# A DeltaNet layer and an MLP on one core: masked copies on half the columns, W1 in narrower pieces, masks in wide operations, and a new order

## The chip, the cores and the metric

The kernel runs on one core of a Trainium2 chip. The core has five engines that run side by side, each through its own list of instructions in order: PE (TensorE, matrix products), DVE (VectorE), ACT (ScalarE), POOL (GpSimd) and SP, which here only issues DMAs. ACT and POOL issue DMAs too. An engine that waits for a semaphore holds up everything behind it in its own list. The metric is the device time of one execution in microseconds; lower is better. Before the change the median of three runs is 508.97 us (507.42 to 509.17).

## The reference, cut to what matters

```python
def _attn_ref(q, k, v, beta):            # B, H, S, D = 4, 8, 768, 48
    k_n = k / (np.linalg.norm(k, axis=-1, keepdims=True) + 1e-06)
    state = np.zeros((B, H, D, D))
    for t in range(S):
        kt, vt, bt = k_n[:, :, t], v[:, :, t], beta[:, :, t, None]
        y[:, :, t] = np.einsum('bhd,bhde->bhe', q[:, :, t], state)
        v_old = np.einsum('bhde,bhd->bhe', state, kt)
        state = state + bt[..., None] * np.einsum('bhd,bhe->bhde', kt, vt - v_old)
    return y

def _moe_ref(x, g_ln, w_ch1, w_ch2):     # x: (4, 768, 384)
    mu, var = mean and variance of x over the last axis
    xn = (x - mu) / np.sqrt(var + 1e-06) * g_ln
    return x + np.maximum(xn @ w_ch1, 0.0) @ w_ch2
```

The 32 heads' outputs of the first part, side by side, are the rows of 384 that the second part takes. `w_ch1` (384 x 1536) and `w_ch2` (1536 x 384) come as 64-bit floats, all else as 32-bit floats.

## The kernel before, in words

The 768 steps of the recurrence are cut into 12 chunks of 64 (C). Within a chunk the recurrence becomes matrix work: with G, the products of the chunk's keys among themselves (`gram`), scaled by beta and the norms, the chunk needs the inverse of a triangular 64x64 matrix for each of the 32 heads (xt). Then `recur` computes the chunk's updates u, its outputs y and the new state, normalises the rows of y (`ln_act`) and transposes them (xnt). `mlp` multiplies by W1, applies the maximum with zero and multiplies by W2; from chunk 1 on the second product, and from chunk 4 on the first too, use schemes with fewer products and more sums (`seven`, `fifteen`).

The inverses are made in two ways. For chunk 0 `first_inverse` does it in six levels of doubling. Heads are taken in two groups g. Level 0 scales G by the factors ndb (L693) and puts its masked elements into a matrix that starts as a copy of the unit matrix (L702, `copy_predicated`), which is transposed on DVE (L708) and copied by ACT (`back`, L679). Each further level n has a product E (L720, 32 products of 64x64), a masked copy of E out of PSUM into another such matrix (L727, mask n), a product Z (L737), transposes of Z (`nat`, L685) and copies of its changed columns (`back`). In level 5 alone E, Z and the masked copy work on half of the columns. For later chunks `rows_inverse` does it by a loop of 31 steps on DVE, each a product and a difference (L856, L863), after its G has gone to DRAM (gd) and come back regrouped (gb), followed by a store (xd), loads of the blocks (xt) and `join`. Chunk 1 has its own loop; from then on two chunks share one.

The masks of the six levels are made in the first microseconds from two iotas, on 64-wide tiles: four operations for xor, eye and rows, and for each level two on the bits (L395, L402) and one that joins them (L408). `first_norms` makes ndb from the squares of k: a sum (L595), a square root (L596), +1e-6 (L597), a product (L598), a reciprocal (L599) and a scaling (L602).

W1 and W2 are loaded as pairs of 32-bit words in 12 pieces of 768 KB on ACT's queue (`fetch`) and turned into 32-bit floats by `convert`: two operations on ACT (L524, L532), a shift on DVE (L529) and a sum on POOL (L542). A piece of W1 is 128 rows by 768 columns, so that a tile of 128 columns of W1 needs three pieces. The first three pieces are converted in halves.

The order of all work is written out: `Line.add` numbers each step, the string ORDER lists the numbers, and each engine's list and each DMA queue follow it. What an engine does next is never decided on the chip.

## Time and profile before

| what | value |
|---|---|
| median of three runs | 508.97 us |
| the profiled execution's own time | 506.83 us |
| its span, first to last instruction | 505.1 us |
| PE busy | 485.9 us (96%) |
| DVE, POOL, ACT busy | 355.2, 275.7, 249.0 us |
| chain that ended last | PE 78%, DVE 13%, SP's queue 3% |
| first L1322 (first product of MLP 0) | 53.1 us |
| rows loop of chunk 1 on DVE | 39.98 to 72.2 us |

Busy times overlap between engines. The clock in the profile is the share of full speed that PE was granted; a group of 32 products of 64x64 takes 0.69 us at full clock and about 1.1 at half. "L693" is a line of the kernel before; durations of single instructions come from the timeline of the one profiled execution.

### The profile page before, as it was taken

The page shows a single profiled execution, that of the slowest core. Times are in us where ns is not written, and L with a number is a line of the kernel's source. Part 1 is how long each engine was busy: PE and PEld are TensorE (multiplying, and loading weights), DVE is VectorE, ACT ScalarE, POOL GpSimd, SP SyncE. Part 2 cuts the span into 40 slices and gives each one's busy share as a digit, 9 for nine tenths or more (in the row PEclk, how much of TensorE's full clock was granted, in tenths as well). Part 3 has the DMA queues.
Part 4 walks back from the last instruction along what each step waited for, and adds up shares of the span by engine and source line. Part 5 has one row for each costly group of instructions (what it writes and reads, how often), then busy time and mean ns, then how long its engine had stood idle before and what let it go on. Part 6 is the DMA issues. An engine that isn't in the chain of part 4 may idle for free.

```text
span 505.1 us, 22184 instructions
## 1 busy us (share of the span) xinstructions
PE 485.9 (96%) x9606; PEld 445.7 (88%) x9606; DVE 355.2 (70%) x774; ACT 249.0 (49%) x620; POOL 275.7 (55%) x430
## 2 busy tenths in 40 slices
PE   6777999999999999999999999999999999999996
PEld 3666988688988898899999999999999999999996
DVE  9689987997699458886559898478899238143251
ACT  5777772633645434636444544436563347363230
POOL 5464527255754595629893462591642851645643
PEclk9776799999999999999999999999999999999999
DMA  8979896756646676448734434765245412111101
GB/s 173 308 153 187 270 189 79 107 138 133 90 87 106 192 127 114 46 100 205 155 41 64 102 55 153 150 91 87 57 85 136 82 23 58 43 50 46 31 12 31
DMA packets 196097, 54.99 MB, mean 109 GB/s; under 512 B 186076, under 2 KB 189404, under 8 KB 196000
## 3 DMA queue, kind: packets, MB, share of 16 engines
q1 hardware_dynamic: 189920, 40.58, 42.1%
q10 hardware_dynamic: 3872, 9.83, 6.1%
q0 software_dynamic: 2208, 3.17, 3.7%
q8 instruction: 75, 1.23, 1.0%
q14 instruction: 22, 0.18, 0.1%
HBM read 36.64 MB, written 16.91 MB: 106 GB/s over the span
## 4 chain that ended last, share of the span: by engine, by line
PE 78%; DVE 13%; SPq 3%; issue 2%; POOL 1%; DMA 1%; ACT 1%; ACTq 0%; DVEq 0%; POOLq 0%
PE f L1419 31%; PE f L1217 22%; PE f L1296 6%; DVE xb L863 4%; DVE tmp L856 4%; SPq L349 3%; PE by L1020 2%; PE two L1013 2%; PE by L979 2%; PE by L771 2%; PE two L979 2%; PE two L1030 1%; PE two L771 1%; PE by L894 1%; PE by L900 1%
## 5 line engine op out<-in xcount | busy, mean ns | idle before, releaser
L1406 POOL TENSOR_TENSOR h_all<-h_all 128x256 f32<-128x256 f32 x123 | 90.2, 746 | 133.3 <-PE f L1419 103.7
L1419 PE MATMUL f<-w_sb,h_all 128*128 128x192 f32 x492 | 109.5, 332 | 0.0
L1419 PE MATMUL f<-words,h_all 128*128 128x192 f32 x396 | 84.5, 330 | 0.3 <-POOL h_all L1406 0.3
L1419 PEld LDWEIGHTS f<-w_sb,h_all 128*128 128x128 f32 x492 | 81.8, 190 | 1.8 <-DVE o L1437 0.2
L863 DVE TENSOR_TENSOR xb<-xb,tmp 128x87 f32<-128x87 f32 (+21 forms) x186 | 73.7, 396 | 4.8
L856 DVE TENSOR_TENSOR tmp<-xb,gb 128x87 f32<-128x87 f32 (+21 forms) x186 | 73.1, 393 | 4.9
L1237 DVE TENSOR_TENSOR h_all<-h_all,f 128x512 f32<-128x512 f32 x96 | 63.6, 682 | 14.2 <-PE f L1217 13.1
L1419 PEld LDWEIGHTS f<-words,h_all 128*128 128x128 f32 x396 | 66.6, 190 | 1.7 <-POOL h_all L1406 1.0
L1296 PE MATMUL f<-xnt,w_sb 128*128 128x256 f32 x216 | 50.2, 382 | 0.0
L349 POOL DMA_DIRECT2D tb<-in_k_dram x64 | 41.9, 660 | 10.3 <-DVE kt L751 9.4
L1239 ACT ACTIVATE h_all<-h_all 128x512 f32<-128x512 f32 x48 | 28.5, 624 | 34.4 <-DVE h_all L1237 34.0
L1296 PEld LDWEIGHTS f<-xnt,w_sb 128*128 128x128 f32 x216 | 40.2, 190 | 5.2
L1233 ACT COPY h_all<-f 128x512 f32<-128x512 f32 x48 | 26.3, 590 | 33.9 <-PE f L1217 17.1
L1437 DVE TENSOR_TENSOR o<-f,x 128x192 f32<-128x192 f32 x33 | 11.6, 352 | 41.8 <-PE f L1419 25.9
L1217 PE MATMUL f<-words,w_sb 128*128 128x128 f32 x256 | 31.7, 276 | 0.0
L1305 ACT ACTIVATE h_all<-f 128x256 f32<-128x256 f32 x36 | 13.4, 383 | 34.8 <-PE f L1296 34.8
L1217 PEld LDWEIGHTS f<-words,w_sb 128*128 128x128 f32 x256 | 30.0, 192 | 0.2
L1217 PE MATMUL f<-xnt,w_sb 128*128 128x128 f32 x192 | 25.4, 276 | 0.0
L542 POOL TENSOR_TENSOR w_sb<-words 128x768 uint32<-128x768 uint32 (+1 forms) x11 | 15.0, 1364 | 17.7 <-DVE words L529 16.7
L1217 PEld LDWEIGHTS f<-xnt,w_sb 128*128 128x128 f32 x192 | 23.7, 192 | 0.1
L1322 PEld LDWEIGHTS f<-xnt,w_sb 128*128 128x128 f32 x144 | 19.5, 203 | 3.4 <-ACT h_all L1330 0.2
L1084 ACT ACTIVATE xnt<-xnt,g_sb 128x256 f32<-128x256 f32 x27 | 12.5, 499 | 19.2 <-DMA xnt<-xld 19.1
(246 smaller groups left out, 955.0 us busy)
## 6 DMA issues: line engine op xcount, KB each, us to landing
words<-in_moe_w_ch_dram ACTq DMA_DIRECT2D x10, 768.0 KB, 7.8
gd<-gsb SPq DMA_DIRECT2D x11, 512.0 KB, 3.9
v<-in_v_dram SPq DMA_DIRECT2D x24, 192.0 KB, 4.2
kr<-in_k_dram SPq DMA_DIRECT2D x46, 96.0 KB, 3.9
out_dram<-o SPq DMA_DIRECT2D x44, 96.0 KB, 2.4
xld<-xlt SPq DMA_DIRECT2D x9, 384.0 KB, 3.0
xnt<-xld SPq DMA_DIRECT2D x36, 96.0 KB, 3.3
gb<-gd SPq DMA_DIRECT2D x44, 64.0 KB, 3.0
```

Source lines behind the costliest of these rows:

```text
L349: add(eng, cost, lambda: QUEUE[eng].dma_start(out=out_, in_=in_), r, w, bulk=n * ns / 16e3, **kw)
L856: lambda j=j, n=n, w=w, t=t: nc.vector.tensor_tensor(out=t, in0=xv[:, 0:n, j : j + 1].to_broadcast([np_, n, w]), in1=gv[:, j : j + 1, j + ...
L863: "DVE", dve(n * w), lambda t=t, rest=rest: nc.vector.tensor_tensor(out=rest, in0=rest, in1=t, op=ALU.subtract),
L979: nc.tensor.matmul(dst[half(e), hp, j], src[drows(hp), (e if n else key_half(c, hp, e)) * GP + j], s_all[drows(hp), e, j], start=(n == 0 o ...
L1217: nc.tensor.matmul(wide(p[:, 128 * n : 128 * n + 128]), w[n // 2][:, n % 2 * 128 : n % 2 * 128 + 128], r, start=start and n == 0, stop=Tru ...
L1233: add("ACT", act(512), lambda: nc.scalar.copy(o, p), pk, ok)
L1237: add("DVE", dve(512), lambda: nc.vector.tensor_tensor(out=o, in0=o, in1=p, op=op), pk, ok)
L1239: add("ACT", act(512), lambda: nc.scalar.activation(o, o, ACTF.Relu), [], ok)
L1296: nc.tensor.matmul(p[:, 0:TOK], w1_sb[:, t, f * 128 : (f + 1) * 128], xnt[:, t], start=(t == 0), stop=(t == KC - 1))
L1322: nc.tensor.matmul(p[:, 0:128], w1_sb[:, t, f * 128 : (f + 1) * 128], xnt[:, t, cols], start=(t == 0), stop=(t == KC - 1))
L1406: add(eng, cost, lambda: e.tensor_tensor(out=out_, in0=x, in1=y, op=op), r, w, port=2 if eng == "Pool" else 1, pr=-2)
L1419: lambda f=f, t=start and f == 0: nc.tensor.matmul(p[:, 0:D2], lhs(f), rhs[:, f], start=t, stop=(f == F2 - 1), skip_group_check=True),
```

## The change

Five things. (1) The masks: the bits of xor and of the row or column number are packed into one word (`both`), shifted by all levels' amounts at once, masked and compared. Mask 0 and masks 1 to 5 are each made in three operations, the packing takes two: 8 where there were 18, and one of the four before them goes, against a small iota on POOL. (2) In levels 2 to 4 E is computed, and the masked copy made, only on the half of the columns that the level changes; the copy is then two instructions, one for each PSUM bank. Z stays whole. (3) A piece of W1 is all 384 rows by 256 columns, so that one piece holds all of two tiles of 128 columns; its rows in DRAM are 2 KB long. (4) In `first_norms` the squared norm is made by ACT (Square with bias 1e-6), beside DVE's +1e-6. (5) ORDER is new from the first step to the last.

```diff
+    c_pool(lambda: nc.gpsimd.iota(steps, pattern=[[1, 6]], base=0, channel_multiplier=0), 0.15, ["steps"])
...
-    for n in MASKED:
-        k_, m, w = n, masks[n], C
-        t1, t2 = (flat[:, C * i : C * i + w] for i in (2 * n, 2 * n + 1))
+    for n, (own, key) in enumerate(((bits, "bits"), (rows_, "rows"))):
         c_dve(
-            lambda t1=t1, k_=k_, w=w: nc.vector.tensor_scalar(
-                out=t1, in0=xor[:, 0:w], scalar1=w - 1, scalar2=k_, op0=ALU.bitwise_and, op1=ALU.logical_shift_right
+            lambda n=n, own=own: nc.vector.scalar_tensor_tensor(
+                out=both[:, n], in0=own, scalar=16, in1=xor, op0=ALU.logical_shift_left, op1=ALU.bitwise_or
             ),
...
+    for n in range(2):
+        ns_ = slice(0, 1) if n == 0 else slice(1, 6)
+        m_ = ns_.stop - ns_.start
         c_dve(
...
+            lambda n=n, ns_=ns_, m_=m_: nc.vector.tensor_tensor(
+                out=wide[:, ns_], in0=both[:, n : n + 1].to_broadcast([128, m_, C]),
+                in1=steps[:, ns_, None].to_broadcast([128, m_, C]), op=ALU.logical_shift_right,
             ),
...
+                out=wide[:, ns_], in0=wide[:, ns_], scalar1=65536 + C - 1, scalar2=None, op0=ALU.bitwise_and
...
+                out=small[:, ns_].bitcast(I32), in0=wide[:, ns_], scalar1=65537, scalar2=None, op0=ALU.is_equal
...
+    WC = WN // KC
     pieces = [
-        (w1_sb[:, t, f : f + WN], w_ch1.bitcast(U32)[t * 128 : (t + 1) * 128, 2 * f : 2 * (f + WN)], ("w1", t, f // WN))
-        for f in range(0, DFF, WN)
-        for t in range(KC)
+        (
+            w1_sb[:, :, f : f + WC],
+            w_ch1.bitcast(U32)[:, 2 * f : 2 * (f + WC)].rearrange("(t p) n -> p t n", p=128),
+            ("w1",),
+        )
+        for f in range(0, DFF, WC)
...
+            add("ACT", 0.21, lambda nr=nr, nd=nd: nc.scalar.activation(nd, nr, ACTF.Square, bias=eps), kn_ + ["eps"], kd, **kw)
             add("DVE", 0.17, lambda nr=nr: nc.vector.tensor_scalar_add(nr, nr, 1e-6), [], kn_, port=2, **kw)
-            add("DVE", 0.17, lambda nr=nr, nd=nd: nc.vector.tensor_tensor(out=nd, in0=nr, in1=nr, op=ALU.mult), kn_, kd, port=1, **kw)
...
         def cols(ap, n, x):
-            return ap.rearrange("p a i (b x l) -> p a i b x l", x=2, l=1 << n)[:, :, :, :, x] if n == 5 else ap
+            if n == 5:
+                return ap.rearrange("p a i (x l) -> p a i x l", x=2)[:, :, :, x]
+            return ap[:, 0].rearrange("p i (b x l) -> p i b x l", x=2, l=1 << n)[:, :, :, x] if n >= LEAST else ap
...
         def col2(ap, n, x):
-            return ap.rearrange("p (b x l) -> p b x l", x=2, l=1 << n)[:, :, x] if n == 5 else ap
+            return ap.rearrange("p (b x l) -> p b x l", x=2, l=1 << n)[:, :, x] if n >= LEAST else ap
...
-                for nr, v, pk in E[4]:
+                for nr, v, pk in E[4] if n < LEAST or n == 5 else [
+                    (slice(a, a + 1), v[:, a - nr.start : a - nr.start + 1], E[2 + a]) for nr, v, _ in E[4] for a in range(nr.start, nr.stop)
+                ]:
```

The numbers in ORDER are step numbers, which the new steps shift, so its lines can't be compared as they stand. Matched by what the steps are, these are the moves that the prediction speaks of:

- ACT: the first fetch of W1 stands right after the two k loads (before: after three copies and two squares), and the first conversion of that piece (L524) right after the squares of k, ahead of the square root, of both copies of kt (L573) and of all else. The fetches of the second and third piece stand after those copies.
- DVE: the pads and masks come first, with the wide shift just before the first sum of squares (L595); both groups of level 0 are scaled, copied and transposed before masks 1 to 5 are compared, and then both level-1 copies follow each other. The shift of W2's first piece (L529) stands ahead of the level-5 copy of group 1 (before: behind u's scaling).
- PE: both G products, then G of chunk 1, then E of level 1 for both groups and Z for both; both E and both Z of level 2 and E of level 3 stand ahead of the first queries product (L771). The second y product and two transposes of chunk 3's keys stand ahead of the first product of MLP 0.
- POOL: W2's first piece is summed ahead of the second half of W1's second piece.
- SP: six loads of q for chunk 2 stand behind the store of xd and the loads of gb (before: ahead of them). The xd store keeps its place between gb loads.
- From chunk 2 on every engine's list has swaps of neighbouring steps; the steps are the same.

74 lines of the change are left out of this document (37 added, 37 removed), and 184 rows, old and new, of the table ORDER.

## The prediction

> **What bounds the kernel now.** I read the page's slices first, then the windows of 10 us, then the chain and the timeline of the opening.
>
> ```profile
> PE   6777999999999999999999999999999999999996
> DVE  9689987997699458886559898478899238143251
> PEclk9776799999999999999999999999999999999999
> ```
>
> PE is full from the fifth slice (50 us) on and has holes before it; its clock is below full only there. The windows give the size:
>
> ```profile
> 0.00:10.00 10.00, 6.95 (x58) 3.47 (x58) 8.98 (x31) 4.18 (x10) 6.60 (x17) 1.00 0.84 137
> 10.00:20.00 10.00, 7.66 (x207) 6.32 (x207) 7.36 (x20) 8.36 (x21) 1.71 (x3) 0.74 1.12 305
> ...
> 40.00:50.00 10.00, 7.69 (x224) 6.87 (x228) 8.76 (x30) 7.85 (x20) 5.13 (x6) 0.60 0.93 166
> 50.00:60.00 10.00, 9.97 (x211) 8.99 (x204) 9.69 (x19) 8.02 (x19) 4.79 (x4) 0.72 0.88 294
> ...
> 150.00:200.00 50.00, 50.00 (x1140) 44.61 (x1133) 34.54 (x82) 20.62 (x54) 33.68 (x54) 1.00 0.66 132
> ```
>
> Of PE's 19.2 us idle (505.1 - 485.9), 14 us lie before 50 us; later there are 0.4 us at 123 us, about 0.3 until 150, and 4.4 after 400, nearly all of it the last sums and stores. So the end moves by as much as the opening does, if PE is then still fed. It is fed through DVE: the chain runs over DVE's rows loop (L856, L863) from 53 to 114 us, then SP's eight DMAs and `xnj` at 123.03, for which PE waits only 0.4 us. A lead must therefore exist on both: PE's opening work, and the point where the rows loop of chunk 1 stands.
>
> Inside the opening, the chain and the timeline:
>
> ```profile
> 3.88 3.28 DVE xb L402 x2
> ```
> ```profile
> 5.93 0.52 ACT L594 ACTIVATE xln<-kr 128x384 f32<-128x384 f32 x1 [2.18 <-DMA kr<-in_k_dram]
> 7.04 0.37 ACTq L349 DMA_DIRECT2D words<-in_moe_w_ch_dram  x1
> 8.10 0.54 DVE L595 TENSOR_REDUCE ksum<-xln 128x8 f32<-128x384 f32 x1
> 11.15 0.68 DVE L693 TENSOR_TENSOR gsb<-two,ndb 128x512 f32<-128x512 f32 x1
> 15.16 0.55 ACT L524 ACTIVATE words<-words 128x384 f32<-128x384 f32 x1
> 18.23 0.76 DVE L727 COPY_PREDICATED gsb<-u,by 128x512 f32<-128x512 int32 x1
> 42.10 0.43 DVE L727 COPY_PREDICATED pt<-u,two 128x256 f32<-128x256 int32 x1
> ```
>
> The squares of k end at 6.45, yet DVE reduces them at 8.10, behind mask work: 1.65 us late. The first scaling of G (L693) comes at 11.15; the second level-1 copy (L727, group 1) ends at 18.99. The last level, already on half the columns, takes 0.43 instead of 0.73.
>
> **The change part by part.** *Masks.* Twenty-two DVE instructions become eleven, and POOL gets one more iota (0.17, L375; its order now has it ahead of the beta DMAs, hidden in the first 2 us). A 64-wide operation has 0.20; the 320-wide ones lie between 64 and larger rows: shift 0.47 (0.21 at 64, 1.24 at 1024), and and compare 0.30 each (0.20 at 64, 0.32 at 384). Together some 2.9 us, against some 7.8 us of busy DVE now, since several were stretched (L402 2.38, L395 1.47). On the path: up to -1.65 for the reduce. At worst nothing, where another wait takes its place.
>
> *Predicated copies, levels 2 to 4.* Six of 0.73 (512 elements) become twelve of 128. The line through 0.73 at 512 and 0.43 at 256 gives 0.28 at 128, so 0.56 a pair: -0.17 each, -0.5 on the chain of one group. Bounds: if short runs of 4 to 16 columns cost what 256 do (0.43), +0.13 each, +0.8 over six; at 0.16, the small operation's row, -0.4 each. I take -0.5, since level 5's row is the same operation.
>
> *E on half the columns.* Nothing: level 5's 32 products of 64x32 took 1.09 and 1.08, the 64x64 ones at the same half clock 1.08. At full clock the 64x64 group takes 0.69 and its weight loads 0.56, so at best -0.13 each.
>
> *Norms.* The multiply (0.16) leaves DVE, a Square (0.2 to 0.3, as L596) joins ACT; the +1e-6 (0.17) leaves the path. Zero, within 0.2.
>
> *W1 in pieces.* Same bytes, same count of fetches and conversions, rows of 2 KB instead of 6. The first fetch moves from 7.04 to ACT's place right after the k loads (about 2.2), and its first conversion (L524) moves ahead of the square root and the two kt copies on ACT. ACT waits there until the whole piece has landed, and behind it wait the norms, PE's first Gram products and so L693. Landing now takes 6.5 to 9.2 us (the `words` rows), so 8.7 to 11.4; then L524 0.55, sqrt 0.3, two kt copies 0.56 with small steps between: PE's Gram product at 10.9 to 13.6, done 0.69 later, and L693 at 11.6 to 14.3 instead of 11.15. The eight k loads and two q loads share the DMA engines with it, already at 1.1 in 4 to 7 us. MLP's own need of W1 starts at 53 us: hidden, with 10 us to spare for pieces 0 and 2; piece 1's second half now follows a W2 piece (1.49) on POOL, near 50, so with 2 us of cover.
>
> *Reordering, level 0 and 1.* Both groups are scaled, copied and transposed before E: 0.68+0.75+0.65+0.73+0.70+0.70 = 4.2 us, then the mask compare 0.3, then both level-1 copies 1.5 with no PE work between. From L693: 6.0 us. Before it was 7.8 (11.15 to 18.99), because Z1, slow at half clock, and G of chunk 1 stood between the E products. So the second copy ends at 17.6 to 20.3, against 18.99: -1.4 to +1.3.
>
> *Reordering, levels 2 to 5.* Z2 of both groups and E3 now stand ahead of the queries product, which held PE for 2.4 us ("issue", 22.17 to 24.58). I follow ACT, which carries the back copies and the W1 conversions: from words0's landing (fetch now at about 13, so 19.7 to 22.3) six back copies, two q copies and a conversion put Z2 at about 24 (24.8 now). Z2 1.1, two transposes 0.8, E3 1.1, then on DVE copy 0.28, W1 shifts 0.33 and 0.55, copy 0.28: Z3 at 28.7 (32.1 now). Z3 1.1 and transposes 0.8; on DVE two scalings of P 1.34, two copies 0.56, a shift 0.55, a copy 0.28, the norms 0.9, a copy 0.28: Z4 at 34.5 (37.1 now). Then the gb scaling and four transposes, 3.1: the loop's first step at 37.6 (39.98 now). But DVE then has a W2 shift (L529, 0.55) ahead of the last level's second copy, and that shift waits for ACT's Prelu, which stands behind the back copies of Z4 and Z5: about 44.1. Behind the shift are the copy, Z5 of group 1 and u. So u's scaling ends near 46.2 (47.5), y0 begins at 46.2 (47.56), and the loop's step of 192 elements is at 46.9 (47.42). What is lost there was won before.
>
> *After the opening.* DVE's rows loop keeps its count; one W2 shift (0.55) now lies before this point rather than after it, another moves behind the loop, and an xnt scaling (0.54) moves into it: net -0.4, so the loop ends 0.9 early. After it, SP's store and seven gb loads (72.2 to 76.9) still end the wait, with the q loads now behind them: 0. PE meanwhile has done the second y0 and two transposes (0.68 and 1.04, 1.7 us of work) before MLP rather than after. From 125 us on the order is new as well; that can hardly win where idle is near zero, and costs 0 to 1.5 (three waits like the 0.58 at 492).
>
> **Sum:** the loop's lead of 0.9 and the 1.4 of y0 pull at the same PE; between them, since some PE work now lies ahead of the loop's results, I take the mean, and the later order at zero: **-1.2 us**. The profiled execution then is 505.6 (now 506.83 = span 505.1 + 1.73); the median stands 2.14 above it, so **507.8 us** against 508.97. The half-percent bound, about what a measurement of this kernel can tell from no change, is 2.5 us.
>
> **The two behaviours behind the spread.** Stretched L402 (2.38, others 0.13 to 0.20) overlaps three POOL copies of 0.62 (L421). The new wide shift stands just ahead of the reduce, with three such copies queued on POOL: if it is stretched like that, 1.9 us, the reduce is no earlier than now. That costs the forecast nothing, as ACT is held to 8.7 anyway, but takes 1.65 from case (a) below. The Trainium skill, "SBUF — State Buffer", Who interferes with whom, says that a VectorE operation with two SBUF inputs and a GpSimd one that reads SBUF exclude each other for a whole instruction; by that rule the stretch would come.
>
> The granted clock is 0.5 at 15 to 21.5, 25 to 31.5 and 42.5 to 55.6 us, in the last spell with PE busy in every microsecond from 48: 7.6 us of dense work before full clock. The Trainium skill, "TensorE: Matmul & The Clock Gate", The HAM clock gate, says that about 3.4 us of sustained work bring it back; by that rule the new kernel's spell would end some 4 us after its dense work begins, and the time would be that of case (c), early; the trace shows it slower.
>
> **The rivals.**
> (a) *The opening gains in full.* The W2 shift isn't late (Prelu ready by 42), so the 2.4 us at the loop's first step survive, with the 0.55 of that shift, done early; if the piece lands early too, the reduce's 1.65 comes on top: -3 to -4.6, 504.4 to 506. For it: the lead at Z3 of 3.4 us; against: ACT is full from 24 to 38 by the sum of its rows.
> (b) *ACT held by the first W1 piece.* Slower than before: the piece contends with the small k and q packets; landing at 11.4 or later gives +1.3 at level 1, delays words0 and everything behind ACT by as much again: +2.6, and +4 with the 1.5 of the later order: 511.6 to 513. It decides from a landing at 10.1 us, 7.9 after issue; the median of the rows is 7.8. Against: landings that long had two other pieces beside them.
> (c) *Clock.* The last half-clock spell ends sooner or later than the opening's lead would have it. For it: the spells before lasted 6.5, so they vary from 6.5 to 13; against: the same operations, in groups of the same size. Half of that difference either way, 3.3 us at half speed, is 1.7 us of PE work: 506.1 (early) or 509.5 (late).
> (d) *Nothing arrives.* The loop, not PE, sets the end, and its lead is lost to stretched steps (L863 1.57, L856 1.55 now): 509.
>
> **How the numbers follow.** Forecast with (d), whose time is inside its range: 0.42. (a) 0.29. (b), with losses in the new later order: 0.20. (c) early 0.05, late 0.04. Of the forecast, 0.02 lies more than 2.5 us slower, by waits after 125. So faster 0.29 + 0.05 = 0.34, same 0.40 + 0.04 = 0.44, slower 0.22. The likeliest case alone: 506.5 to 509.5. The range of 8 in 10 leaves out the best of (a) and the worst of (b), a tenth each: 504.6 to 511.9.
>
> **What would show it.** Right: the reduce at 6.5 to 7; L693 at 11.6 to 12.5; second level-1 copies ending at 17 to 18.5; 128x128 predicated copies at 0.25 to 0.30; E of 64x32 no shorter than weight loads; PE idle before 50 us near 13 us. Wrong: ACT idle over 3 us before its first L524; the wide shift over 1 us; PE idle in 100 to 130 us; a half-clock spell past 57 us; waits of over 1 us between 130 and 490.

## The result, and the profile after

The changed kernel takes **512.39 us** (median of 20 runs, 509.37 to 516.31) against 508.99 us (20 runs, 505.85 to 510.75): a ratio of 1.0075, 95% interval 1.0058 to 1.0092. It is slower by 3.4 us. The forecast was 507.8, its range ended at 511.9; the time that came is that of rival (b), 511.6 to 513. The profiled execution took 511.42 us, 1 us under its median, with a span of 509.6 us, 4.5 more than before's 505.1.

The page's slices (40 equal parts of the span, tenths busy; the last row is the granted clock):

```profile
PE   5758899998999999999999999999999999999996
DVE  3787896997789539987749898559989336244251
PEclk9985999999899999999999999999999999999999
```

The first slice shows a late start: DVE at 3 where it had 9, PE at 5 where it had 6. The windows of the profile after (busy us of PE, weight loads, DVE, ACT and POOL with counts in brackets, then clock, DMA share, GB/s):

```profile
0.00:10.00 10.00, 4.43 (x13) 1.78 (x13) 2.33 (x13) 4.52 (x7) 6.48 (x19) 1.00 0.84 163
40.00:50.00 10.00, 8.23 (x194) 7.07 (x190) 7.02 (x22) 6.12 (x15) 4.49 (x5) 0.55 1.01 210
50.00:60.00 10.00, 8.03 (x330) 7.13 (x324) 9.66 (x23) 8.54 (x23) 5.67 (x8) 1.00 0.78 218
125.00:150.00 25.00, 22.89 (x654) 21.02 (x655) 18.40 (x44) 12.97 (x38) 9.90 (x16) 0.93 0.56 78
```

In the first 10 us DVE works 2.33 us (8.98 before) and PE runs 13 products (58 before). PE is idle for 25.6 us in all, 19.2 before; 1.97 of it now lie in 50 to 60 us and 2.11 in 125 to 150, where there were 0.03 and 0.27. PE's busy time is 1.9 us less: the opening's last half-clock spell ends near 49 us rather than at 55.7, mean clock 0.983 against 0.973. So rival (c)'s early clock came in this execution, and bought nothing: PE waited instead. It was this execution's luck: over all 20 executions the mean clock has a median of 0.976 (0.961 to 0.986), and over 31 of the kernel before, run beside the first experiments, 0.975 (0.964 to 0.978). A new half-clock spell of 3.4 us lies at 127.6 to 131.0 (the 0.93 in the last window, 1.00 before).

The loss starts in the opening. Its timeline (start, duration, engine, line, operation, count; in brackets the idle time before it and what ended it; ACTq and SPq are DMA issues):

```profile
0.80 7.83 SPq L349 DMA_DIRECT2D kr<-in_k_dram  x7
2.25 0.64 ACTq L349 DMA_DIRECT2D h_all<-in_moe_w_ch_dram  x1
9.38 0.94 ACT L605 ACTIVATE xln<-kr 128x384 f32<-128x384 f32 x2 [2.53 <-DMA kr<-in_k_dram]
9.66 0.39 PE L590 MATMUL f<-ident,u 16*64 16x8 f32 x6 [2.85 <-DMA u<-in_beta_dram]
9.93 0.55 DVE L606 TENSOR_REDUCE ksum<-xln 128x8 f32<-128x384 f32 x1 [6.59 <-ACT xln L605]
10.22 0.54 ACT L542 ACTIVATE h_all<-h_all 128x384 f32<-128x384 f32 x1
15.41 0.69 DVE L706 TENSOR_TENSOR gsb<-by,ndb 128x512 f32<-128x512 f32 x1 [1.43 <-PE by L646]
21.17 0.74 DVE L742 COPY_PREDICATED gsb<-u,two 128x512 f32<-128x512 int32 x1 [0.63 <-PE two L733]
```

The first piece of W1 is issued at 2.25. SP's seven k loads take 7.83 us to issue (5.10 for the same seven in the run late_fetch below, which has that fetch later), the squares of k begin at 9.38 instead of 5.93, and the transposes of k on PE stand behind the beta products, which wait for beta until 9.66. The conversion of the piece (L542, at 10.22) shows no wait of its own: by then the piece had landed. What came late was k and beta.

"Step 192" below is the loop's step of 192 elements on DVE; `xnj` is the second transpose of that name, that of chunk 2's inverse (the first, chunk 1's, is at 83.78 before and 85.83 after). Both are starts.

| stage (us) | forecast | before | after |
|---|---|---|---|
| reduce of the squares of k | 6.5 to 7 | 8.10 | 9.93 |
| first scaling of G (L693, now L706) | 11.6 to 14.3 | 11.15 | 15.41 |
| second level-1 copy ends | 17.6 to 20.3 | 18.99 | 21.91 |
| Z2 | 24 | 24.8 | 26.24 |
| Z3 | 28.7 | 32.1 | 30.81 |
| Z4 | 34.5 | 37.1 | 37.20 |
| first step of chunk 1's loop | 37.6 | 39.98 | 39.38 |
| level-5 copy, group 0 | | 42.10 | 42.06 |
| W2 shift (L529, now L547) | 44.1 | | 47.89 |
| u's scaling begins | | 46.94 | 49.19 |
| y0 (L1020, now L1035) | 46.2 | 47.56 | 50.17 |
| step 192 | 46.9 | 47.42 | 50.60 |
| chunk 1's loop ends | | 72.16 | 73.96 |
| `xnj` | | 123.03 | 126.28 |
| span less `xnj` | | 382.1 | 383.3 |

Against the forecast the chain is 1.8 to 2.7 us late from Z2 to the loop's first step and 3.7 late at step 192. Against the kernel before it has made up the late start by Z3, and the loop's first step and the level-5 copy of group 0 are as early as before. The 3.2 us at step 192 arise between 42 and 50.6 us. Four lines show where, three of the kernel after and, last, the back copies of late_fetch:

```profile
42.06 0.44 DVE L742 COPY_PREDICATED pt<-u,two 128x256 f32<-128x256 int32 x1 [0.34 <-PE two L733]
43.28 0.83 ACT L692 COPY xt<-f 64x128 f32<-64x128 f32 x3 [2.73 <-POOL w_sb L553]
47.89 0.56 DVE L547 TENSOR_SCALAR words<-words 128x768 uint32<-128x768 uint32 x1 [1.94 <-ACT words L542]
```

```profile
41.02 0.83 ACT L692 COPY xt<-f 64x128 f32<-64x128 f32 x3
```

ACT stands 2.73 us in front of a W2 fetch, with back copies of the inverse behind it. The list names POOL's sum, but in the trace's records the fetch counts on the same semaphore (number 107) as a k load that SP issued at 34.44; that load lands at 42.71, and ACT's wait for the semaphore ends at 42.73. Behind the back copies stands ACT's Prelu, for which DVE's W2 shift waits 1.94 us; behind the shift are the level-5 copy of group 1, u, and the loop's steps. In late_fetch SP issued that load at 32.06, and ACT issued the fetch at 39.72 without a wait.

After step 192 the difference falls to 1.8 us at the end of chunk 1's loop, is 3.25 at `xnj`, and 1.2 more come behind it. Differences of this size in single traces must be read with care: new_to_130 below has the changed kernel's order up to 125 us and an `xnj` at 125.34, 0.9 us earlier; old_to_130 and old_order, with one order up to there, are 1.5 apart (123.00 and 124.48). At step 192 these pairs agree within 0.3 us.

### The profile page after: what moved, and what is told of

It is laid out like the page before. It is cut to its first block, busy times and chain, and to the rows that moved or that the text cites. A ratio compares the mean times of both kernels' runs of the same rounds, so it can differ in the third digit from the quotient of the medians.

```text
span 509.6 us, 22168 instructions
## 1 busy us (share of the span) xinstructions
PE 484.0 (95%) x9606; PEld 443.4 (87%) x9606; DVE 352.5 (69%) x767; ACT 250.2 (49%) x623; POOL 278.7 (55%) x431
## 4 chain that ended last, share of the span: by engine, by line
PE 82%; DVE 5%; DMA 4%; ACT 3%; POOL 3%; issue 2%; SPq 1%; ACTq 0%; POOLq 0%; DVEq 0%
PE f L1434 30%; PE f L1232 22%; PE f L1311 6%; PE f L1337 3%; PE by L1035 2%; PE two L994 2%; PE two L1028 2%; PE by L786 2%; DVE tmp L871 2%; PE by L994 2%; PE f L1352 2%; PE two L1045 2%; PE two L786 1%; DVE xb L878 1%; SPq L349 1%
## 5 line engine op out<-in xcount | busy, mean ns | idle before, releaser
L1434 PE MATMUL f<-words,h_all 128*128 128x192 f32 x396 | 87.4, 333 | 0.3 <-POOL h_all L1421 0.3
L871 DVE TENSOR_TENSOR tmp<-xb,gb 128x87 f32<-128x87 f32 (+21 forms) x186 | 76.2, 410 | 4.6
L878 DVE TENSOR_TENSOR xb<-xb,tmp 128x87 f32<-128x87 f32 (+21 forms) x186 | 75.1, 404 | 4.5
L1311 PEld LDWEIGHTS f<-xnt,w_sb 128*128 128x128 f32 x216 | 40.1, 190 | 5.4 <-ACT xnt L1122 0.4
L1232 PE MATMUL f<-words,w_sb 128*128 128x128 f32 x256 | 32.4, 277 | 0.0
L1232 PEld LDWEIGHTS f<-words,w_sb 128*128 128x128 f32 x256 | 30.2, 192 | 0.3
L1232 PE MATMUL f<-xnt,w_sb 128*128 128x128 f32 x192 | 25.1, 275 | 0.0
L1232 PEld LDWEIGHTS f<-xnt,w_sb 128*128 128x128 f32 x192 | 23.5, 192 | 0.1
L1208 POOL TENSOR_TENSOR words<-xnt 128x128 f32<-128x128 f32 x32 | 15.3, 486 | 13.8 <-ACT xnt L1099 13.7
```

Source lines behind the costliest of these rows:

```text
L871: lambda j=j, n=n, w=w, t=t: nc.vector.tensor_tensor(out=t, in0=xv[:, 0:n, j : j + 1].to_broadcast([np_, n, w]), in1=gv[:, j : j + 1, j + ...
L878: "DVE", dve(n * w), lambda t=t, rest=rest: nc.vector.tensor_tensor(out=rest, in0=rest, in1=t, op=ALU.subtract),
L1208: "Pool", 0.47, lambda: nc.gpsimd.tensor_tensor(out=o, in0=x, in1=y, op=op), xk + yk, ok,
L1232: nc.tensor.matmul(wide(p[:, 128 * n : 128 * n + 128]), w[n // 2][:, n % 2 * 128 : n % 2 * 128 + 128], r, start=start and n == 0, stop=Tru ...
L1311: nc.tensor.matmul(p[:, 0:TOK], w1_sb[:, t, f * 128 : (f + 1) * 128], xnt[:, t], start=(t == 0), stop=(t == KC - 1))
L1434: lambda f=f, t=start and f == 0: nc.tensor.matmul(p[:, 0:D2], lhs(f), rhs[:, f], start=t, stop=(f == F2 - 1), skip_group_check=True),
```

## The experiments

The runs are read by step 192, `xnj`, and span less `xnj`. The medians are over all executions of a run; "before" is the kernel before on the same chip in the same batch.

### The place of the first fetch, from both sides: early_fetch and late_fetch

early_fetch is the kernel before with its own first W1 fetch (6 KB rows) moved right behind ACT's k loads, and nothing else:

```diff
 L349 DMACopy kr_89<-in_k_dram 64x8x48 x2
+L349 DMACopy words_66<-in_moe_w_ch_dram 128x1536
 ...
 L573 TensorCopy kt_72<-by 128x4x2x64
-L349 DMACopy words_66<-in_moe_w_ch_dram 128x1536
```

> The kernel before with one thing moved: its own first W1 fetch, 768 KB in rows of 6 KB, stands right behind the two k loads of ACT (about 2.2 us) instead of at 7.04. Theory A (the place of the fetch, not the form of the piece): the squares of k start at 8 to 9.5 us instead of 5.93, L693 at 13 to 14.5 instead of 11.15, and the time rises by 1.5 to 3.5 us, to 510.5 to 512.5. Rival D (the pieces of 256 columns do it, three times as many rows of 2 KB): the squares stay at 6 to 6.8, the time within 0.7 of 509.0. Rival B (a lag in the opening is caught up with): squares late, time within 0.7 of 509.0.

late_fetch is the changed kernel with that fetch moved back behind the first copy of kt, and the piece's three conversions moved back too, behind back copies of level 0:

```diff
 L349 DMACopy kr_89<-in_k_dram 64x8x48 x2
-L349 DMACopy h_all<-in_moe_w_ch_dram 128x3x512
 ...
 L605 Activation xln<-kr_89 128x384 x2
-L542 Activation h_all<-h_all 128x3x128
 L607 Activation knrm_121<-ksum_119 128x8
 L584 TensorCopy kt_72<-by 128x4x2x64
+L349 DMACopy h_all<-in_moe_w_ch_dram 128x3x512
```

> The changed kernel with one thing moved: the first W1 fetch stands behind the first kt copy on ACT instead of right behind the k loads, and the three conversions of that piece (two Prelu, one multiply) stand behind the back copies of level 0. Theory A (the early fetch holds up the k and beta loads on the DMA engines, and the opening's lag comes from there): the squares of k start at 5.9 to 6.5 us instead of 9.38, the first scaling of G (L706) at 11 to 12.5 instead of 15.41, the second level-1 copy ends at 17.5 to 19 instead of 21.91; the time falls to 508 to 510.5, as far as a later hold at 40 to 48 us lets the lead through. Rival B (the opening's lag is caught up with anyway and the loss of 3.4 us arises after 40 us): L706 comes as early, but u and y0 (49.19 and 50.17 us) move by under 0.7 us and the time stays at 511.5 to 512.5. Rival C (it is the conversion on ACT ahead of the norms, not the loads): the squares stay at 9.4.

early_fetch: 510.40 us against 509.06 (ratio 1.0052, 1.0015 to 1.0089), span 507.3. late_fetch: 510.76 against 509.06 (1.0027, 0.9998 to 1.0055), span 507.8. The squares of k in the timeline, of early_fetch first and then of late_fetch:

```profile
9.08 0.53 ACT L594 ACTIVATE xln<-kr 128x384 f32<-128x384 f32 x1 [4.64 <-DMA kr<-in_k_dram]
```

```profile
6.37 0.94 ACT L605 ACTIVATE xln<-kr 128x384 f32<-128x384 f32 x2 [0.19 <-DMA kr<-in_k_dram]
```

One moved DMA instruction delays the squares from 5.93 to 9.08 in the old kernel, and moving it back, with the conversions, brings them from 9.38 to 6.37 in the new one. The DMA views of the first 10 us of the kernel after and of late_fetch (count, size, median us from issue to landing) say the same of k:

```profile
kr<-in_k_dram SPq DMA_DIRECT2D x7, 96.0 KB, 6.8
```

```profile
kr<-in_k_dram SPq DMA_DIRECT2D x7, 96.0 KB, 4.0
```

PE's wait for beta ends at 7.19 in late_fetch and at 9.66 in the changed kernel.

What this costs is known less well than that it happens. In ratios the early place costs the old kernel 0.52%, 2.6 us (0.8 to 4.5 by the interval), and the late one gives the new kernel 1.0075 - 1.0027 back, 2.4 us of the 3.8 that the ratio makes. By medians it is 1.3 and 1.7: three of early_fetch's ten executions took 513.8 to 515.7 us, the others 509.0 to 511.1. early_fetch has W1 in the old pieces, so it isn't their form.

Nor does the delay go through whole. In early_fetch 3.15 us at the squares are 1.75 at the loop's first step (41.73) and 1.5 at step 192 (48.95). In late_fetch the lead over the changed kernel is 3.05 us at the first scaling (12.36) and 1.6 at the end of level 1 (20.28), after a pause of PE of 2.06; at Z2 (26.24), Z3 (31.02), Z4 (37.75) and the loop's first step (39.93) there is none. At u (47.80) and step 192 (49.24) it is 1.4 again, since ACT's wait before the W2 fetch has gone.

The Trainium skill, "DMA: Bandwidth & Descriptors", Queues, rings and completion order, says that each DMA engine takes its queues in turn, a packet of some 9 to 17 descriptors from one before it goes to the next; with 768 KB in large rows in one queue and k in rows of 192 bytes in another, that goes with what is seen here (k lands 6.8 us after issue beside it, 4.0 without). How the engines share their time within a load isn't in these traces.

### The rest of the opening: late_beta, hold_fix, repaired

late_beta is late_fetch with the transposes of k ahead of the beta products on PE:

```diff
 L568 Matmult f_132<-u 128x512 x2
+L579 Matmult by<-ident,kr_89 128x128 x8
 L590 Matmult f_129<-ident,u 64x8
 ...
-L579 Matmult by<-ident,kr_89 128x128 x8
```

> As the run late_fetch, and besides PE's eight small products of beta stand behind the eight k transposes of chunk 0 instead of ahead of them. Theory M (in the changed kernel PE waited at 9.66 for beta, which comes over POOL's queue, before it took k, so that the place of these products is a second reason for the late start): the k transposes start at 6.0 to 6.8 instead of 7.51 in late_fetch, the first scaling of G (L706) at 10.8 to 11.8 instead of 12.36, the time falls by 0.4 to 1.2 us against late_fetch, to 509.6 to 510.4. Rival N (the start is then set by the kt copies on ACT or by the norms on DVE): L706 at 12 to 12.6, the time within 0.4 of late_fetch's 510.76.

510.77 us against 508.56 (1.0041, 1.0020 to 1.0063), span 509.4: nothing won, although the opening did what was hoped. The transposes of k came at 6.30 (7.51 in late_fetch), the first scaling at 10.21, and the second level-1 copy ended at 18.25, 0.74 ahead of the kernel before. The loop's first step was still 1.7 ahead (38.28). ACT stood twice:

```profile
19.22 0.57 ACT L542 ACTIVATE words<-words 128x384 f32<-128x384 f32 x1 [2.81 <-DMA words<-in_moe_w_ch_dram]
41.60 0.83 ACT L692 COPY xt<-f 64x128 f32<-64x128 f32 x3 [2.24 <-DMA tb<-in_k_dram]
```

At 16 us it stands in front of a conversion whose piece hasn't landed; that was made up. At 39 us it stands in front of the W2 fetch that waits for SP's k load (landed 41.03, wait ended 41.05, semaphore 107 again), with back copies (L692) behind, and u came at 47.51, 0.6 later than before, step 192 at 48.92, 1.5 later. PE was idle 5.4 us less than in the changed kernel but busy 5.1 us more, with the clock at half from 24.3 to 55.0.

hold_fix takes the changed kernel as it is and mends only 40 to 50 us:

```diff
 ACT
-L349 DMACopy words_68<-in_moe_w_ch_dram 128x2x768
 ...
 L692 TensorCopy xt_84<-by 128x4x2x16
+L349 DMACopy words_68<-in_moe_w_ch_dram 128x2x768
 DVE
+L742 CopyPredicated pt_79<-u,by 128x2x4x32
 ...
+L1016 TensorTensor u<-two,bnat 128x2x4x48
 L547 TensorScalarPtr words_67<-words_67 128x768
 ...
-L742 CopyPredicated pt_79<-u,by 128x2x4x32
-L1016 TensorTensor u<-two,bnat 128x2x4x48
```

E of level 5 for group 1 also goes ahead of a group of key transposes on PE.

> The changed kernel, its first fetch left early; reordered only between 40 and 50 us: on ACT the back copies of level 4 of both groups go ahead of a W2 fetch; on PE E5 of group 1 goes ahead of the kt transposes of chunk 2; on DVE the last level's second copy and u's scaling go ahead of the W2 shift, and POOL's addition follows that shift. Theory A2 (this stretch adds a hold of its own to the opening's lag): ACT's idle 2.7 us at 40.5 goes, Z5 of group 0 starts at 42 to 43 instead of 43.93, u's scaling at 46.3 to 47.6 instead of 49.19, and the time falls by 1 to 2.2 us, to 510.2 to 511.4. Rival E (what was put back makes the W2 additions and the later fetches late, or DVE's rows loop sets the end whatever u does): u is early, but the time stays within 0.6 of 512.4.

513.20 us against 509.06 (1.0068, 1.0037 to 1.0099), span 511.6: no gain. k was late again (squares at 8.47). The hold itself went: from Z4 to u it took 10.2 us instead of 12.0. But Z4 came 2.0 later (39.22), so that u was at 49.37, and the moved W2 shift now stood between u and the loop's next steps: from u to step 192 it took 3.04 us, 1.41 in the changed kernel. Why Z4 came later isn't settled.

repaired puts together late_beta, the W1 conversions behind Z1's back copies, the W2 fetch behind Z4's, E of level 5 earlier, and the W2 shift behind step 192.

> The run late_beta with two more edits to its order. First, the four W1 conversions that stand on ACT between level 0 and level 1 go behind Z1's back copies and the q copies, and their two shifts on DVE behind the level-2 copies; in late_beta ACT stood 2.8 us at 19.2 for a piece to land. Second, Z4's back copies of both groups go ahead of the W2 fetch (ACT stood 2.24 us at 41.6 behind that fetch, which itself waited for a k load to land), E5 of group 1 goes ahead of the kt transposes, and the W2 shift goes behind the loop's step of 192. Theory S (these two holds on ACT are what eats the lead that late_beta had at 18 us, 0.74 us ahead of the kernel before): E2 at 20.5 to 21.5 instead of 22.95, u's scaling at 44.5 to 46.5 instead of 47.51, the step of 192 at 45.5 to 47.5 instead of 48.92, the time 507 to 509.2. Rival T (the work put back comes due at once on another engine, or PE's issue stalls and half clock take the lead): u after 46.8 or the step of 192 after 48, the time over 509.8.

510.74 us against 509.55 (1.0031, 1.0012 to 1.0050), span 507.5. u came at 46.80, as early as before (46.94), step 192 at 48.00, the best of the new order but 0.6 us behind the kernel before, and `xnj` at 124.50. Before 30 us PE stood 2.49, 1.50 and 0.91 us with no releaser but "issue".

Z4 to u is the stretch that holds the wait for the W2 fetch. It took 12.0 us in the changed kernel, 12.1 in new_to_130 and 11.4 in late_beta, which have that wait; 10.1 in late_fetch, 10.2 in hold_fix and 10.7 in repaired, which don't; 9.8 in the kernel before.

### The parts by themselves: masks_halves, masks_halves_late, halves_only, pieces_only

masks_halves is the kernel before, in its own order and with its own W1 pieces, with the wide masks and the half-column E and copies.

> The kernel before, with the wide bit masks (in its own order, each wide step where the first of the old ones stood) and with E and the predicated copies of levels 2 to 4 on half of the columns, each copy as two of 128 elements in one place; W1 pieces, fetches, norms and all the rest of the order as before. Theory F (these two parts are good for what the forecast gave them, and the loss comes from the W1 fetch and the order): the reduce of ksum at 6.5 to 7.2 instead of 8.10, L691's first scaling of G 0.5 to 1.5 us earlier than 11.15, copies of 0.27 to 0.30; the time 506.8 to 508.6. Rival G (the parts gain nothing, since other waits take their place: the kt copies on ACT, the queries product's stall): 508.6 to 509.5. Rival H (they cost, by broadcast reads that stretch beside POOL or by the second copy's own overhead): over 509.8.

510.52 us against 509.06 (1.0023, 0.9993 to 1.0053), span 509.2. The reduce came at 6.74, as the prediction wanted for the masks, and yet the first scaling of G fell from 11.15 to 13.67. The timeline of masks_halves:

```profile
9.89 3.04 DVE L604 TENSOR_SCALAR knrm<-knrm 128x8 f32<-128x8 f32 x1
9.95 0.94 POOL L838 MEMSET xb<- 64x1024 f32 x1 [2.32 <-DVE u L415]
10.00 2.92 DVE L606 RECIPROCAL ndb<-ndb 128x8 f32<-128x8 f32 x1
10.85 1.16 POOL L428 COPY xt<-u 128x512 f32<-128x512 f32 x2
11.95 0.94 POOL L1547 MEMSET tb<- 128x1024 f32 x1
```

POOL waits for the last mask, since the masks' scratch tile is the one that it clears for the rows loop. With the masks done early it clears at 9.95 rather than at 18.29, and an addition on 8 elements a row takes 3.04 us instead of 0.16: it ends, with the reciprocal, when POOL's four instructions in a row are done. masks_halves_late tests this by one move on DVE:

```diff
 L604 TensorScalarPtr knrm_121<-knrm_121 128x8
-L415 TensorScalarPtr u<-xb 128x320
 L605 TensorTensor ndb<-knrm_121 128x8
 ...
 L711 CopyPredicated kt_74<-u,gsb_80 128x2x256
+L415 TensorScalarPtr u<-xb 128x320
 L738 CopyPredicated gsb_82<-u,two 128x2x256
```

> The kernel before with the wide masks and the half-column copies and E, as in the run masks_halves, but with one step moved: the compare that finishes masks 1 to 5 stands just ahead of the first level-1 copy instead of between the small steps of the norms. POOL's clearing of xb waits for that compare, and behind it stand two copies and another clearing. Theory I (in masks_halves POOL's 3 us of work, set free at 9.9 us, stood beside the norms' small DVE steps and stretched an addition and a reciprocal to 3 us): these steps take 0.2 us each, the first scaling of G (L702) starts at 9.8 to 11 us instead of 13.67, the time falls to 507 to 508.8. Rival J (the stretch has another cause, or the order of the rows loop takes the gain back): L702 stays over 12.5, or the time stays at 509.5 to 510.5.

508.04 us against 508.56 (0.9990, 0.9963 to 1.0016), span 504.8. POOL clears at 14.50, the addition is back at 0.16 and the first scaling is at 10.62:

```profile
9.57 0.16 DVE L604 TENSOR_SCALAR knrm<-knrm 128x8 f32<-128x8 f32 x1
10.62 0.68 DVE L702 TENSOR_TENSOR gsb<-two,ndb 128x512 f32<-128x512 f32 x1
14.50 0.94 POOL L838 MEMSET xb<- 64x1024 f32 x1 [6.88 <-DVE u L415]
```

`xnj` comes at 122.05 rather than 126.24. The Trainium skill, "SBUF — State Buffer", Who interferes with whom, says that a `tensor_scalar` can enter a mode in which it and GpSimd lock each other out of a shared pair of ports for a whole instruction. The addition is one; the section doesn't name the reciprocal. The trace goes further, for DVE got no turn between four of POOL's instructions.

halves_only is the kernel before with the half-column E and copies alone.

> The kernel before with E and the predicated copies of levels 2 to 4 on half of the columns alone, each copy as two of 128 elements; masks, W1 and the rest of the order as before. Forecast's term: 0.17 us less for each of six pairs, 0.5 us on the chain of one group, nothing for E: 508.2 to 509.0. Rival K (the copies' gain stays in waits of the level chain, for PE and ACT): 508.7 to 509.3. Rival L (products that write every other run of 4 to 16 columns, or two copies where one was, cost more than they save): over 509.8.

508.94 us against 508.56 (1.0007, 0.9979 to 1.0034), span 504.6. Step 192 comes at 46.02 and `xnj` at 121.81, 1.2 to 1.4 us ahead of the kernel before, and the time is the same: PE is idle 2.4 us less, but its busy time grows from 485.9 to 487.8. The mean clock of the two profiles is 0.973; over all executions it has a median of 0.967 here and 0.975 beside it.

pieces_only is the kernel before with W1 in pieces of 256 columns; nine late steps had to be put later than their old places, since a sum that the old pieces left free now has to come first.

> The kernel before with W1 fetched and converted in pieces of 256 columns (rows of 2 KB) instead of rows of 6 KB, with every fetch and conversion in its old place; where W1's storage is used again late in the kernel, nine steps that would have run ahead of their new conditions stand somewhat later. Theory O (the form of the pieces is harmless; only where the first fetch stands costs): 508.6 to 509.8, the landing of the words fetches 6 to 9.5 us as before. Rival P (three times as many rows make the landings longer, and ACT's conversions and the back copies behind them wait): landings over 10 us, 510 to 512.

514.47 us against 508.56 (1.0101, 1.0050 to 1.0152), span 513.2. The opening is nearly untouched (first scaling 11.99, step 192 at 47.94, `xnj` at 123.82), and 7 of the 8 us come after it, with two waits of PE of 2.1 and 1.9 us in the list of waits from 130 us on; PE is also busy 5.6 us more, at a mean clock of 0.965. So the new pieces lose in the old order, more than either recorded expectation said. That it is the order they force, and not their form, is likely (old_to_130 has them and loses less), but not shown.

### New order against old: old_opening, old_to_130, old_order, new_to_130

These four have the changed kernel's code and mix the two orders. old_opening has before's order for the first 328 steps (to 53 us), then after's; old_to_130 for 816 steps (to about 125 us); old_order all through, with twelve sums of W1 on POOL 10 to 17 steps earlier, which the new pieces demand; new_to_130 has after's order for 804 steps, then before's, with the same twelve sums earlier. In short, with both lists matched by what a step does:

```diff
-ORDER: after's steps, 1 to 2988
+old_opening: before's 1 to 328, then what is left, as in after
+old_to_130:  before's 1 to 816, then what is left, as in after
+old_order:   before's 1 to 2988, twelve sums (L1178) earlier
+new_to_130:  after's 1 to 804, then what is left, as in before, twelve sums earlier
```

> The changed kernel's code (masks, half-column copies, norms, W1 in pieces of 256 columns) with the kernel before's order for the first 328 steps, up to the first MLP product (about 53 us), its fetches and conversions included, the compare of masks 1 to 5 just ahead of the first level-1 copy; from there on the changed kernel's order. Theory Q (the loss is the new order of the opening, the early fetch with it; the parts and the order after 55 us are harmless): squares of k at 5.8 to 6.4, u's scaling at 45.5 to 47.5, the loop's step of 192 elements at 46 to 48, xnj at 121.8 to 123.5, the time 507.2 to 509.3. Rival R (the pieces of 256 columns, or the order after 55 us, cost by themselves, as the run pieces_only with 514.5 would have it): u as early, but PE waits of over 2 us in sum after 125, the time over 510.

513.44 us against 509.55 (1.0074, 1.0051 to 1.0097), span 512.5. Step 192 is back at 48.69, but from there to `xnj` it took 80.5 us where all others took 74.6 to 76.9: where the two orders meet, DVE waits 2.5 us for ACT. It says nothing about the parts.

> The changed kernel's code with the kernel before's order for the first 816 steps, to about 125 us (the second xnj), and from there the changed kernel's order; the compare of masks 1 to 5 just ahead of the first level-1 copy. In the run old_opening the seam of the two orders lay at 53 us, and 4.9 us were lost in the rows loop behind it; here it lies where the loop is over. Theory Q (the new order of the opening is the loss; W1 in pieces, the norms and the order after 125 us are harmless): u's scaling at 45.5 to 47.5, xnj at 121.5 to 123.5, 508 to 509.5. Rival U (the order after 125 us costs by itself what was left after the fetch was moved back, about 1.4 us): xnj as early, but PE idle over 1.5 us in 125 to 200 us, 509.8 to 511. Rival P (the pieces cost in the opening, by fetches that land later): u's scaling after 48.

510.65 us against 508.50 (1.0034, 1.0009 to 1.0058), span 509.2. Step 192 at 47.44 and `xnj` at 123.00 are those of the kernel before (47.42 and 123.03), with the changed code: what the changed kernel loses in the opening is order, not code. (old_order, with the same order up to here, has 47.73 and 124.48, so the second time is good to about 1.5 us.) But span less `xnj` is 386.2, and the timeline of old_to_130 shows 2 us of it:

```profile
130.09 1.30 POOL L349 DMA_DIRECT2D tb<-in_k_dram  x2
132.03 1.29 POOL L349 DMA_DIRECT2D tb<-in_k_dram  x2
133.33 1.19 POOL L1421 TENSOR_TENSOR h_all<-h_all 128x256 f32<-128x256 f32 x1
134.57 0.59 PE L1434 MATMUL f<-words,h_all 128*128 128x192 f32 x2 [2.06 <-POOL h_all L1421]
```

POOL issues four loads ahead of a sum that PE waits for. Whether that is the new late order or the place where the orders meet, this run can't tell. The next two look at that.

> The changed kernel's code (masks, half columns, Square on ACT, W1 pieces) with the whole of the order of before; twelve sums of W1 on POOL, which the new pieces tie to the first product that reads them, are done 10 to 17 steps earlier. Theory W (the code costs nothing, the new order costs all 3.4 us): xnj at 122.5 to 123.5, span less xnj 382 to 383, median 508 to 509.5. Rival X (the code itself, above all the pieces of 256 columns, costs after 125 us): xnj as above, but span less xnj at 385 or more, with waits of over 1 us between 130 and 300, and 511 to 513.

> The changed kernel with its own order for the first 804 steps (to about 125 us) and the order of before from there on, with the same twelve sums earlier. Theory Y (the new order after 125 us costs the 1.25 us by which the changed kernel falls behind after xnj): xnj at 126.3 as in the changed kernel, span less xnj back from 383.3 to about 382, median 511. Theory Z (all is lost before 126 us, and the rest is the spread of single profiles): span less xnj at 383 or more, median 512 to 512.8.

old_order: 514.55 us against 508.53 (1.0122, 1.0093 to 1.0151), span 512.7. new_to_130: 520.90 against 508.53 (1.0257, 1.0224 to 1.0290), span 518.7. Both are slower than either of their expectations, neither answers its question, and both show why in the same line, here of old_order:

```profile
237.35 0.72 POOL L1178 TENSOR_TENSOR w_sb<-w_sb 128x256 f32<-128x256 f32 x1
238.03 1.68 POOL L1208 TENSOR_TENSOR words<-xnt 128x128 f32<-128x128 f32 x4
239.36 2.08 PE L1232 MATMUL f<-words,pt 128*128 128x128 f32 x8 [3.45 <-POOL words L1208]
```

The twelve sums hold POOL from 229.6 to 238.0, and PE waits 3.45 us for what stands behind them, in both kernels. In old_order the other 4 us have to do with the clock: PE is idle for 22.4 us, 3.45 of them here, so 19 as before, but it is busy for 490.3 us instead of 485.9, at a mean clock of 0.966 instead of 0.973. new_to_130 doesn't win back the 1.2 us after `xnj`: PE loses 5.0 us in 125 to 150 (2.1 in the changed kernel), 2.6 of them waiting for DVE's `rstd`. Before's late order fits the changed opening less well than the changed one does.

### The pauses of PE: shifted

PE stands now and then with no releaser but "issue", 0.2 to 4.3 us, mostly in the opening. Counted from the start, the pauses come after product records 220 or 221, 347, 474, 601 and so on, 126 to 128 apart; late_fetch shows seven in a row, other kernels only some of them. Counted with PE's weight loads and semaphore instructions, late_fetch's lie 255 or 256 records apart. If the count makes them, 64 more records ahead must move a pause to another place in the chain. shifted is masks_halves_late with 32 products of one column, of no use, in PE's first filler (64 records):

```diff
+            for _ in range(small):
+                nc.tensor.matmul(ps[:, 0:1], nought, nought[:, 0:1])
-        fill(1, 512, f_[3], FK[3], pr=-100)
+        fill(1, 512, f_[3], FK[3], small=0 if n else 32, pr=-100)
```

> The run masks_halves_late with 32 products of one column more in PE's first fill, 64 records and as many weight loads, which nobody waits for (PE has nothing else before 6 us). In all runs PE has stood still, waiting for nothing that is shown, at the same places of its program, 126 or 127 product records apart: in masks_halves_late after 30 records of the first Z1 (0.83 us), 22 of the first queries product (2.51), 18 of Z3 (0.38), 7 of the first v product (0.56). Theory V (PE's program arrives in blocks of this many instructions): the pauses stand 64 records earlier in the order, the first at the end of the Gram product of chunk 1 or in the first E1, the second after about 22 records of the second Z1, the third in Z2 or E3; the time moves by under 1.5 us either way, less if pauses fall where PE waits for DVE anyway: 506.5 to 509. Rival W (they belong to these products or to what the other engines do then): the pauses stay in Z1, the queries product, Z3 and the v product.

532.33 us against 508.50 (1.0454, 1.0418 to 1.0490): as a timing the run failed, since the 64 records took 13.65 us and held up everything. As a count it answered. Two lines of PE's timeline in shifted:

```profile
3.50 13.65 PE L566 MATMUL f<-u 128*128 128x1 f32 x64
38.17 0.42 PE L731 MATMUL by<-qt,gsb 64*64 64x32 f32 x11 [0.98 <-issue]
```

In masks_halves this pause stands in the queries product, ahead of the last 10 of its 32 records; here it stands in E of level 2, ahead of the last 11 of 32, which is 64 records earlier in the list, give or take one. A second one agrees: a pause after 7 records of the v product in masks_halves_late comes here after 8 of level 5's first Z, 63 records earlier. The other three pauses of masks_halves_late didn't show here. So an order also decides which step a pause hits; in the first 60 us the pauses add up to 3.2 us in the kernel before and 6.0 in the changed one. What PE does in them isn't shown by any of these traces.

## Why the prediction was wrong, and where it was right

**The step that failed** is the paragraph on the W1 pieces. It moved the first fetch from 7.04 to 2.2 and priced the landing of the piece, 8.7 to 11.4, and its conversion on ACT. It said in one sentence that eight k loads and two q loads share the DMA engines with it, already at 1.1 in 4 to 7 us, and then gave those loads no delay. They were late by 3.45 us at the squares, beta by 2.5 (against late_fetch), and the first scaling came at 15.41, 1.1 past the late end of the forecast's 11.6 to 14.3. That the place of the fetch does this is shown from both sides; it costs some 1.3 to 2.6 us.

**A second step failed with it**, in the paragraph on levels 2 to 5: "What is lost there was won before". The W2 shift was priced at 44.1, from the rows that stand ahead of Prelu on ACT. It came at 47.89, because ACT had stood 2.73 us for a k load that SP issued late. The loop's first step had its forecast lead over before cut from 2.4 to 0.6, and that wait took more than the rest.

**Rival (b)** had the right instruction, the right sign and nearly the right time, with the wrong victim: it held ACT for the piece, from a landing at 10.1 us. The piece was there when ACT came to it at 10.22; ACT, DVE and PE had waited for k. The bound from the landings of other pieces was aimed at the wrong transfer.

**The masks.** The eight operations are as short as estimated (the wide shift 0.48 us, with no stretch), and the reduce could come at 6.74, as masks_halves shows. In the changed kernel this is worth nothing, as DVE stands idle for 6.59 us waiting for the squares. (Of L402 before, the prediction says 2.38 and others 0.13 to 0.20; one more, at 6.10, took 1.06.) "Up to -1.65, at worst nothing" was too kind on the other side: in the old order the early masks cost 2.5 us at the first scaling, by setting POOL's clearing free. The prediction feared the ports for the wide shift; it was the small additions and the reciprocal that were held.

**Predicated copies and E.** Right: the 128-element copies take 0.27 to 0.30, and E of 64x32 takes 0.67 at full clock against 0.69. halves_only has a lead of 1.2 to 1.4 us at step 192 and `xnj`, more than the 0.5 of one group.

**Level 0 and 1.** The term of 6.0 us from the first scaling to the end of the second level-1 copy measured 6.5 (15.41 to 21.91). Only its start was wrong.

**Levels 2 to 4.** The spacing was about right: Z2, Z3 and Z4 came 2.2, 2.1 and 2.7 us later than forecast, when level 1 was already 1.6 us past the late end of its range.

**The loop** of chunk 1 was to end 0.9 us early, 0.4 of it by fewer other steps on DVE. It ended 1.8 late, but from step 192 to its end it took 23.36 us against 24.74, so that this term was too small. **After 125 us**, "0 to +1.5" held: +1.2. But span less `xnj` is 382.1 to 383.0 in the runs with before's late order and pieces (before, early_fetch, masks_halves, masks_halves_late, halves_only) and 382.6 and 383.0 in late_fetch and repaired, with the new one. Nothing there shows a cost of the new late order by itself; the changed kernel, hold_fix and late_beta, with 383.3 to 383.9, each have a half-clock spell of 3.4 us near 130 us that the others lack.

**What stays open.** Of the 3.4 to 3.8 us, 1.3 to 2.6 belong to the early fetch. What the new order loses without it, 1.2 to 2.2 us by the medians of late_fetch, late_beta and repaired, has no single cause here. repaired has neither the late k nor the wait for the W2 fetch, is level with before at u and 0.6 behind at step 192, and is still 0.31% slower. The clock is a rival that no run tries by itself: over all executions its median is 0.970, 0.965 and 0.966 in those three, against 0.973 to 0.975 of the kernel before beside them. An estimate: 0.0055 to 0.010 of 508 us is 2.8 to 5.1 us of PE at full speed, more than what is missing, if PE had work all that time.

**A faster kernel?** The best is masks_halves_late, 508.04 against 508.56, which can't be told from the kernel before. Its `xnj` is 1 us earlier, and PE is idle 2.0 us less than before but busy 1.6 us more; halves_only shows the same, 2.4 and 1.9. So in these two a shorter opening turned PE's idle time into busy time and hardly into a shorter kernel.

## What to carry to other kernels

When a large transfer is moved ahead, price the small ones that are already in flight beside it, not its own landing alone: here 768 KB issued 5 us earlier cost the first loads 3 us, though nobody waited for the 768 KB. Then follow the lists behind those loads to every engine that waits on them, as far as the wait at 43 us. An instruction that becomes free early sets free what waits for it on other engines; ask what that collides with. Two versions of a long written order can't be spliced to find which half is better: each half counts on the lead that its own first part gives.

## What the runs showed of the hardware

- POOL's instructions back to back kept DVE out throughout: an addition on 128x8 took 3.04 us, a reciprocal 2.92, beside a memset, two copies and a memset on POOL.
- PE pauses every 126 to 128 product records (255 or 256 of PE's records in all, in late_fetch), 0.2 to 4.3 us, and in shifted the place moved with the count of records ahead of it.
- Records of products of one column with 128x128 fp32 weights, one after another, took 0.21 us each in shifted (64 in 13.65 us); those of 128 columns in MLP (L1232) keep PE busy for 0.13 each in the changed kernel (256 in 32.4 us).
- Two DMAs that two engines issue can count on one semaphore, and the later then waits for the earlier to land: the W2 fetch on ACT and a k load on SP, both on number 107, landed and released at 42.71 and 42.73 in the changed kernel, 41.03 and 41.05 in late_beta. It held everything behind it on ACT for 2.73 and 2.24 us.
- The half-clock spells lasted 3.4 us or a multiple of it: 6.8, 6.8 and 13.7 in the kernel before, 13.7 and 3.4 in the changed one, 30.7 in late_beta's opening.
